# Block-sparse attention with a gated feed-forward: the first fifth of a written-out instruction order replaced, and six operations exchanged between ScalarE and VectorE

## The chip, the cores and the metric

One core of a Trainium2 chip (trn2). The metric is device time in microseconds (us) of one execution. Engines are named as in the profile: PE is TensorE (PEld its weight loads), ACT is ScalarE, DVE is VectorE, POOL is GpSimd, SP is SyncE. A name such as L757 is line 757 of the kernel.

## The reference

Four batches, 8 heads, 768 tokens, head size 64. A token block has 32 tokens, so there are 24 blocks; a mask lets a query block see its neighbours, the first and the last block, and three sampled blocks.

```python
scores = scale * np.matmul(q, k.transpose(0, 1, 3, 2))
mask = np.abs(blk_i - blk_j) <= 1
mask = mask | (blk_i == 0) | (blk_j == 0) | (blk_i == 23) | (blk_j == 23)
# ... and the three sampled key blocks of each query block
attn = softmax(np.where(mask, scores, -1e9))
x = (attn @ v), heads side by side: 768 x 512 for each batch
h = np.maximum(x @ w_in, 0.0)                 # 512 -> 1024
conv_out = 3-tap convolution of h along the tokens, weights conv_w per feature
gate = 1.0 / (1.0 + np.exp(-conv_out))
out = (h * gate) @ w_out                      # 1024 -> 512
```

## The kernel before

**Attention.** Heads are worked in pairs (P = 0 to 15, four to a batch). For each pair the transposed K and Q stand in two bf16 tiles, `e` (even token chunks) and `o` (odd ones), 64 rows of data and 24 rows of mask (rows 64 to 87), so that one matmul with 88 rows gives scores with the mask added. `e0` and `o0` are the first pair's; there are five such slots. The pairs 0 to 4 get K and Q by loads, a transpose on PE (L470 for K, L508 for Q) and copies out of PSUM by ACT (L328) or DVE (L330); later pairs by DMA transposes into `stg` and copies from there (L330). V goes through a copy `vt<-vn` into a tile with a column of ones.

The work is cut into 144 units of 8 score blocks. Each has two score steps on PE (L746, into one of two PSUM tiles `st`), one exponential on ACT (L757, `pt<-st`, 128x1024) and two steps of attention times V on PE (L779, `av<-vt,pt`). With two `st` tiles, the scores of unit u can start only after the exponential of unit u-2. After 18 units (half a batch's queries, four pairs) DVE divides (L696, L698), the result is transposed (on PE at L717 for the first half batch, by DMA later), and the feed-forward of this half batch begins.

**Feed-forward.** PE multiplies with `winb` (L895) into two small PSUM tiles `mix`; each of the 8 feature chunks of a half batch is then taken out with a relu by ACT (L915) or DVE (L917) into `hE`. DVE multiplies by the three taps (L949) and adds (L959), ACT takes a tanh (L998), DVE adds one (L1001) and multiplies by h into `gT` (L1006). PE multiplies `gT` with `woutb` (L825) into the same `mix` tiles, and DVE or ACT copies the result to `o2s` (L330, L328), from where it is stored. Transposes of K and Q, the relu and the output thus share the two `mix` tiles.

**The first microseconds.** DVE builds the mask: `nblk` (L280) and its scaled copies (L300), `hit` (L276, L284), `may` (L286), and the K rows of the mask in `e0` (L314); these rows are copied to the other head and to `o0` and the other slots (L330, 24 rows). K and Q of pair 0 come in float32 (`o2s1`, `o2s2` for the two heads' K, `o2s0` for Q in two halves) and are cast to bf16 into `nat3` (L328 on ACT or L330 on DVE, for the other engine's form). PE runs 45 matmuls without use (L1027, `warm`) before and between, and 12 later ones (L1034, fill).

**diag.** Four operations of three instructions each (L390) make diagonal matrices of the taps for two feature chunks each; only the last stretch of the kernel uses them.

**What sets the order.** The kernel makes a graph of 1789 operations and then puts them down in the order of a table of two-character numbers, `ORDER`. Where an operation may run on two engines, a letter behind its number says which (A is ACT, V is DVE); another character picks its buffer:

```python
o = ops[64 * CODE.index(line[x]) + CODE.index(line[x + 1])]
x += 2
engines = list(o.alts)
e = engines[0]
if len(engines) > 1:
    e = ENGINES[line[x]]
    x += 1
for b in o.allocs:
    b.index = CODE.index(line[x])
    x += 1
```

Each engine takes its instructions strictly in this order and waits for others through semaphores. There are no priorities at run time.

Of the kernel before, what the change touches and what calls it, by code (L numbers as in the profile page):

```python
# [17 lines left out]


ORDER = """  # L20
000x010z020B0407080905060b1e00a1f1c01q11s11801m11t1E21G21H030y0e0c0gV0d0nV0f0A0i0hA0WA30UA0oAr41r5r6r7r8r9rarb
rcrdrerfrgrhrirjrkrlrmrnrorprqrrrsrtrurvrwrx0Y01210ZA014A0VA13A0mA0XV0jV0+V0lV0t0uryrzrArBrCrDrErFrGrHrIrJrK
15017A16ArLrM4n04o0/14s14t1g11j04p00q10V0p11V1hV11lV1kV4u11dV01iV4x04yrN0rOrPrQ4C14D4z2rRrSrTrUrVrWrXrY4H04I
4E34J44q14r4v4w4Q14R4S54A4B4F4G0s0r1rV14V04W4K1u04X64+14/5071x11vV21yV1zV4L0530544T4U4Y4Z5c15d510E15505e10C1wV
4M01FV24N0F0k5h05i1I0525j21JV35m15n5o31L1561NV575811MV5r05s5f15g5w15x1KV1911n00I5t45y55F05G1bV591S30O0P0Q0R46
1A0470S481O1490T4a1U44b1V4c2404d2634e271TV34f2c14g2e04h2f4i2k24j2m11aV1oV0N1pV5H65k5l5p5q5K15L5M75u5v5z5P05Q
5A05I4O15R05U15V5W15J5a05N610625O5S5T5X5Y6324PV00J5bV5B20D5C5Z35+661675D15EV6416b06c5/0651B160V0K1DV1CV6836d4
0w0v6g16hhq0hr6i56l06m6n6ht1hu6t16uhsV0hvVhO0hQhP6v7hI0hJ6y06zhw1hxhKA6A0hyVhRhS6D16E69hz0hA6F16a1P16e6f6j6I0
6k6J6ohBA1QVhW11RVhT6q0hX6r6K26Q1hF06RhGhC1hD6S3hEAhHVhU6V06W6+11W06p06/6X47056w6x6B73074hL1hM781756hNA796C6G
7a77g06H6L6M6T17h6U6Y1Z17i07l17m6Z717276777q07r7b7n1hYhZi221XV41YVi3i4h+hV06N1i5ia36O1+Vh/ib7d21/V25V4i0ic7ei6  # L30
7s27v17w7c0ii07jio17kid7D07E7x37o7p7t7u7y7z7F4i76s1280292g12h6P7f7I17J7N07G17H7O7A37K5i17P67Biei8i92aV02bVifig
ih2dV02iV17Cijip7S17Tiq7X07Lik7U77Y7M7Q7R831847Vir7Z0851880897Wil8d18e7+8a22jVisV04k2n4l2s34mimV18002lV12tV281
iu18i08j8f38k4ix0iyizV8q18riviwViS4iTiUiV8v08wiA0iBiD1iE8s58x6iCAiFAi+0iW2o22p2qV22rV2u2002v22x2w8A18B7/08F086
878GiG08b8c8g8hiJ1iH8C78H0iXiIA8l8m8t18K18L8S08T8uiK2108yj08n1i/8oj122ViLV23Vj61j28M18U28z8X18Y8D8E8I8J90091
# [1035 lines left out]
```

## Time and profile before

| | |
|---|---|
| time, median of 3 runs | 204.63 us (204.57 to 204.76) |
| span of the profiled execution | 202.8 us, granted TensorE clock 0.998 |
| busy, share of the span | PE 97%, ACT 94%, DVE 90%, POOL 28% |
| exponentials (L757) | 144, mean 1039 ns from start to end |

The profiled execution is given by its span, from the first to the last instruction; the 1.9 us by which the timed runs are longer (204.63 less 202.76) lie around it. Busy time of an engine counts each instruction from its start to its end; neighbours on ACT and DVE overlap by about 0.1 us, and matmuls are pipelined, so a row "x8" in the timeline tells more than a mean duration. A timeline row has the start, the length, the engine, the line, the tiles (written, then read) and, in brackets, how long the engine was idle ahead of it and for whom.

### The profile page before, as it was taken

To read this page: it belongs to the slowest core of one execution; us is meant where nothing else is said; L and a number is where in the kernel's file an instruction comes from. 1 tells how busy PE (TensorE), PEld (TensorE's weight loads), DVE (VectorE), ACT (ScalarE), POOL (GpSimd) and SP (SyncE) were. 2 spreads that over 40 slices of the span, in tenths; PEclk is the share of its full clock that TensorE was granted. 3 is DMA by queue.
4 is the path that set the end of the run, shared out by engine and by line. 5 is a ranking of instruction groups with operands and counts; after the bars stand their busy time and mean duration, and the time that the engine had idled before them with its cause. 6 is when DMAs were issued, how large, how long until landed. Compare 5 with 4: busy or idle time off the path is not lost.

```text
span 202.8 us, 6814 instructions
## 1 busy us (share of the span) xinstructions
PE 196.8 (97%) x2708; PEld 153.9 (76%) x2708; DVE 181.8 (90%) x572; ACT 189.7 (94%) x251; POOL 57.5 (28%) x112
## 2 busy tenths in 40 slices
PE   7899999999999999999999999999999999999993
PEld 7799977986788777877688877876678877876742
DVE  7999989999999979999899988999899968999950
ACT  6999999999999999999999998999999989998842
POOL 8870568630520354202534328400000000000000
PEclk9999999999999999999999999999999999999999
DMA  6999999999998399956869699994321202001515
GB/s 143 177 223 207 182 135 132 167 171 151 155 122 129 61 141 154 213 106 132 133 108 159 82 197 218 135 176 115 124 72 24 41 14 68 13 10 60 204 63 202
DMA packets 53655, 25.96 MB, mean 128 GB/s; under 512 B 39616, under 2 KB 50584, under 8 KB 53624
## 3 DMA queue, kind: packets, MB, share of 16 engines
q0 software_dynamic: 19984, 11.24, 43.7%
q1 hardware_dynamic: 33208, 13.87, 34.6%
q8 instruction: 21, 0.34, 0.7%
q10 hardware_dynamic: 432, 0.43, 0.6%
q14 instruction: 10, 0.08, 0.1%
HBM read 23.08 MB, written 6.29 MB: 145 GB/s over the span
## 4 chain that ended last, share of the span: by engine, by line
PE 78%; ACT 15%; issue 3%; DVE 2%; DMA 1%; ACTq 0%
PE st L746 25%; PE mix L895 18%; PE mix L825 17%; PE av L779 14%; ACT pt L757 11%; DMA o2s<-in_k_dram 1%; DVE e L330 1%; ACT m L998 1%; PE mix L810 1%; PE st L825 1%; PE av L970 1%; ACT nat L328 1%; PE mix L508 1%; ACT hE L915 0%; ACT o2s L328 0%
## 5 line engine op out<-in xcount | busy, mean ns | idle before, releaser
L757 ACT ACTIVATE pt<-st 128x1024 bf16<-128x1024 f32 x144 | 140.6, 1039 | 1.8 <-PE st L746 0.9
L779 PE MATMUL av<-vt,pt 128*128 128x65 bf16 x1152 | 59.9, 193 | 0.2 <-DVE vt L330 0.2
L779 PEld LDWEIGHTS <-pt 128*128 128x128 bf16 x1152 | 52.3, 97 | 9.9 <-issue 0.3
L895 PE MATMUL mix<-xT,winb 128*128 128x384 bf16 (+2 forms) x288 | 53.6, 308 | 0.1
L949 DVE TENSOR_SCALAR m<-hE,cw 128x382 bf16<-128x382 bf16 (+2 forms) x192 | 49.3, 316 | 0.5 <-ACT hE L915 0.2
L825 PE MATMUL mix<-woutb,gT 128*128 128x512 bf16 x176 | 47.1, 379 | 0.3 <-DVE gT L1006 0.3
L746 PE MATMUL st<-o 88*128 88x128 bf16 (+1 forms) x240 | 43.9, 229 | 0.4 <-ACT pt L757 0.3
L746 PE MATMUL st<-o,e 88*128 88x128 bf16 (+1 forms) x228 | 43.4, 233 | 0.0
L746 PE MATMUL st<-e,o 88*128 88x128 bf16 (+1 forms) x224 | 42.3, 234 | 0.2 <-ACT pt L757 0.2
L746 PE MATMUL st<-e 88*128 88x128 bf16 (+1 forms) x208 | 40.9, 239 | 0.1
L746 PEld LDWEIGHTS <-o 88*128 88x128 bf16 x464 | 34.7, 97 | 7.7 <-issue 0.8
L746 PEld LDWEIGHTS <-e 88*128 88x128 bf16 x436 | 33.0, 97 | 7.1 <-issue 0.4
L959 DVE TENSOR_TENSOR m<-m 128x764 bf16<-128x764 bf16 (+2 forms) x64 | 33.5, 532 | 0.4
L895 PEld LDWEIGHTS <-winb 128*128 128x128 bf16 x288 | 24.0, 97 | 8.0 <-issue 0.5
L998 ACT ACTIVATE m<-m 128x764 bf16<-128x764 bf16 (+2 forms) x32 | 26.3, 829 | 0.5 <-DVE m L959 0.3
L825 PEld LDWEIGHTS <-gT 128*128 128x128 bf16 x184 | 15.0, 97 | 9.3 <-DVE gT L1006 0.5
L417 POOL COPY pace<-pt 1x1 bf16<-1x1 bf16 x24 | 6.2, 257 | 49.9 <-ACT pt L757 49.8
L1006 DVE TENSOR_TENSOR gT<-m,hE 128x764 bf16<-128x764 bf16 (+3 forms) x36 | 18.0, 510 | 0.5
L698 DVE TENSOR_TENSOR xtok<-av,rcp 128x384 bf16<-128x384 f32 (+2 forms) x36 | 18.2, 506 | 0.3
L915 ACT ACTIVATE hE<-mix 128x384 bf16<-128x384 f32 (+2 forms) x36 | 17.7, 507 | 0.7 <-PE mix L895 0.5
L240 POOL DMA_DIRECT2D nat<-in_q_dram x23 | 16.8, 733 | 3.2 <-issue 2.5
L917 DVE TENSOR_SCALAR hE<-mix 128x384 bf16<-128x384 f32 x28 | 15.3, 549 | 2.6 <-PE mix L895 2.2
(84 smaller groups left out, 157.4 us busy)
## 6 DMA issues: line engine op xcount, KB each, us to landing
out_dram<-o2s SPq DMA_DIRECT2D x23, 256.0 KB
vn<-in_v_dram POOLq DMA_DIRECT2D x16, 192.0 KB, 5.0
nat<-in_k_dram POOLq DMA_DIRECT2D x15, 192.0 KB, 4.7
nat<-in_q_dram POOLq DMA_DIRECT2D x7, 192.0 KB, 5.2
winb<-in_moe_w_in_dram POOLq DMA_DIRECT2D x2, 512.0 KB, 9.5
woutb<-in_moe_w_out_dram POOLq DMA_DIRECT2D x4, 256.0 KB, 8.2
nat<-in_q_dram POOLq DMA_DIRECT2D x8, 96.0 KB, 4.5
nq<-in_q_dram POOLq DMA_DIRECT2D x5, 96.0 KB, 5.2
```

What stands on the lines that cost most here:

```text
L240: return op(name, {eng: occ}, lambda e: on(e).dma_start(out=dst(), in_=src), prio, deps, dma=(kind, service), **kw)
L698: nm = op("norm", {"DVE": t_dps(128 * C)}, lambda e: nc.vector.tensor_tensor(out=xtok_t[xk.index][:, 0:C].rearrange("p c h d -> p h c d"), ...
L746: nc.tensor.matmul(out=st[:, 128 * x:128 * (x + n_)], lhsT=QK[kc % 2][s][0:88, 1, hh, kc // 2, :], rhs=QK[par][s][0:88, 0, hh, idx:idx + n ...
L757: nc.scalar.activation(out=pt_t[ptb.index], in_=st_t[stb.index], func=AF.Exp, bias=0.0, scale=0.125)
L779: nc.tensor.matmul(out=o[:, off:off + 65], lhsT=pt_t[ptb.index][:, 128 * x:128 * x + 128], rhs=V_t[vslot_b[P].index][:, hh, kc, 0:65], sta ...
L825: nc.tensor.matmul(out=acc(), lhsT=gT_t[gb.index][:, ffc, 128 * t:128 * t + 128], rhs=woutb[:, ffc, :], start=(ffc == 0), stop=(ffc == NFF ...
L895: nc.tensor.matmul(out=mix_t[hb.index][:, w1 * y:w1 * y + w1], lhsT=winb[:, fc, 128 * ffc:128 * ffc + 128], rhs=xT_t[xt_buf[n].index][:, f ...
L915: i = nc.scalar.activation(out=dst, in_=src, func=AF.Relu, bias=0.0, scale=0.5)
L949: i = nc.vector.tensor_scalar(out=m_t[cb.index][:, x, y, 0:w], in0=hE_t[heb.index][:, f0 + y, t0 + x:t0 + x + w], scalar1=cw[:, x, f0 + y: ...
L959: nc.vector.tensor_tensor(out=m[:, a_, :, 0:w], in0=m[:, a_, :, 0:w], in1=m[:, b_, :, 0:w], op=ALU.add)
L998: th = [op("tanh", {"ACT": t_act(2 * w) + 0.04}, lambda e, cb=cb, w=w: nc.scalar.activation(out=m_t[cb.index][:, 0, :, 0:w], in_=m_t[cb.in ...
L1006: i = nc.vector.tensor_tensor(out=gT_t[gtb.index][:, f0:f0 + 2, t0:t1], in0=m_t[cb.index][:, 0, :, 0:w], in1=hE_t[heb.index][:, f0:f0 + 2, ...
```

## The change

Fourteen rows of the table are rewritten: all that runs up to about 46 us of the program on PE and up to about 55 us on DVE. Behind that, each engine's order is the one before. POOL and SP keep their order throughout. Six operations change engine:

- from ACT to DVE: the cast of the first half of pair 0's Q (`nat3<-o2s0`), the copy of the mask rows of Q to the other head in `o0`, the copy of 128 columns of Q from PSUM (`o0<-av0`), and one relu of a 128x384 tile from PSUM (the fifth feature chunk of the first half batch, L915 before, L917 now);
- from DVE to ACT: the cast of the second head's K (`nat3<-o2s2`) and the copy of the mask rows of Q to the other head in `e0`.

Two rows of the table, before and now:

```diff
-000x010z020B0407080905060b1e00a1f1c01q11s11801m11t1E21G21H030y0e0c0gV0d0nV0f0A0i0hA0WA30UA0oAr41r5r6r7r8r9rarb
+040708090005060b1e00a1f1c01q11s1011801m11t1E20e1G2021Hr41r5r6r7r8r80hAr903rarb0gVrcrd0crerfrg0nA0drhrirj0yrkrlrm
...
```

On DVE at the start of the program, from the last step ahead of the sampled blocks to the first copies of the finished K mask (`hit`, `may`: the mask's tables; `o2s`: pair 0's K and Q in float32), before:

```order
L276 TENSOR_SCALAR hit_141<-near_142,ident24_136 24x22
L330 COPY e0_67<-e0_67 24x384
L284 TENSOR_TENSOR hit_141<-colidx_i_140,sbi_139 24x72
L286 TENSOR_REDUCE may_143<-hit_141 24x24
L370 MEMSET vt3_80 128x12
L314 TENSOR_SCALAR e0_67<-may_143 24x24x6 x2
L314 TENSOR_SCALAR e0_67<-may_143 24x8x6
L314 TENSOR_SCALAR e0_67<-may_143 24x2x8x5
L330 CAST nat3_88<-o2s2_127 128x384
L330 COPY o0_72<-e0_67 24x384
```

and of the change, the same stretch:

```order
L276 TENSOR_SCALAR hit_141<-near_142,ident24_136 24x22
L370 MEMSET vt1_78 128x12
L330 CAST nat3_88<-o2s0_125 128x192
L284 TENSOR_TENSOR hit_141<-colidx_i_140,sbi_139 24x72
L286 TENSOR_REDUCE may_143<-hit_141 24x24
L314 TENSOR_SCALAR e0_67<-may_143 24x24x6 x2
L314 TENSOR_SCALAR e0_67<-may_143 24x8x6
L314 TENSOR_SCALAR e0_67<-may_143 24x2x8x5
L330 COPY o0_72<-o0_72 24x384
L330 COPY o0_72<-e0_67 24x384
```

A cast of half of Q now stands ahead of the sampled-block steps where a mask copy stood, and behind the K mask a mask copy stands where the cast of K stood.

On ACT, from its last mask row to the first exponentials, before:

```order
L298 ACTIVATE o0_72<-nblk_138 24x256
L328 CAST nat3_88<-o2s1_126 128x384
L328 CAST nat3_88<-o2s0_125 128x192
L328 COPY o0_72<-o0_72 24x384
L328 COPY e0_67<-mix0_65 64x384
L328 COPY o0_72<-mix1_66 64x128
L328 CAST nat3_88<-o2s0_125 128x192
L328 COPY e0_67<-mix1_66 64x256
L328 COPY o0_72<-e0_67 24x384
L328 COPY o0_72<-av0_63 64x128
L328 COPY e0_67<-av0_63 64x256
L757 ACTIVATE pt0_96<-st0_61 128x1024
```

and of the change:

```order
L298 ACTIVATE o0_72<-nblk_138 24x256
L328 COPY e0_67<-e0_67 24x384
L328 CAST nat3_88<-o2s1_126 128x384
L328 CAST nat3_88<-o2s2_127 128x384
L328 COPY e0_67<-mix0_65 64x384
L328 COPY e0_67<-mix1_66 64x256
L328 COPY o0_72<-mix1_66 64x128
L328 COPY o0_72<-e0_67 24x384
L328 CAST nat3_88<-o2s0_125 128x192
L757 ACTIVATE pt0_96<-st0_61 128x1024
L328 COPY e0_67<-av0_63 64x256
L757 ACTIVATE pt1_97<-st1_62 128x1024
```

One mask copy stands ahead of the first cast, and the last copy of Q has moved behind the first exponential.

On DVE at the end of the first half batch's gates (`m3`, `gT0`: the gate of the last two feature chunks; `stg`: the next pairs' K and Q), one piece of the difference:

```order
 L330 COPY e0_67<-stg0_82 64x1536
 L330 COPY o0_72<-stg0_82 64x1536
+L390 TENSOR_SCALAR diag_131<-ident_135,cw_134 128x128 x3
 L1001 TENSOR_SCALAR m3_121<-m3_121 128x2x382
 L1006 TENSOR_TENSOR gT0_123<-m3_121,hE0_116 128x2x382
+L390 TENSOR_SCALAR diag_131<-ident_135,cw_134 128x128 x3
 L330 COPY vt0_77<-vn1_93 128x12x64
 L330 COPY e1_68<-stg1_83 64x1536
```

Two of the four diag operations stand here now; a third follows between the first two relus of the next half batch, and one is left where all four were, ahead of the first half batch's feed-forward.

More of the change, by code (lines that the diff above doesn't have):

```diff
@@ L20 @@
 ORDER = """
-000x010z020B0407080905060b1e00a1f1c01q11s11801m11t1E21G21H030y0e0c0gV0d0nV0f0A0i0hA0WA30UA0oAr41r5r6r7r8r9rarb
[L22 to L34, printed above, removed]
+040708090005060b1e00a1f1c01q11s1011801m11t1E20e1G2021Hr41r5r6r7r80hAr903rarb0gVrcrd0crerfrg0nA0drhrirj0yrkrlrm
@@ new lines @@
+0WA3rn0UV0XArorp0frqrrrsrt0i0Y00oVru1210jVrv0lV0ZA013A14Arwrx0mA0t0uryrz0/10A10VrArBrCrDrErF0VA0+V11VrG4n04orH
+rI4p0150rJrKrLrM4s117V4t16A4x04yrN00z1g11j0rO0qrP0p4u10B4z21hV14C14DrQ1kV1lVrR0x4H01dV0rS4I4q14E3rTrU4J44r1iV
+4v0s1rV14Q1rV4R4w1u04V04W4S5rW4A4B4+11vV2rX4/4X6rY1x14F0r5301yV544G1zV5074K0C5504L04T1wV4M05c11S35d4U4Y4Z0E1
+1FV25e15h00O4N5i51520F5j21I05m15n1L11JV30P0Q1NV1MV56571KV0R5815r0465s5f15g5o3591911A05w11TV35x470S485t41n01O1
+490T4a5k1U44b1V5F00K4c5G2405l5p4d2635y55q1oV4e1bV1aV5u275K15L4f5H65M75v5z2c15A04g5B22e04h5C5P02f5Q4O10k4PV05I
@@ new lines @@
+5R04i2k25J5U14j5V5N5D11pV5O2m15a05W15bV0w610620D0v5S5T5EV5X5Y661632671B16b06c5Z35+5/01DV1CV64168360V656d46g16h
+hq06i5hr6l06mhsV0ht1hu6t16u6n6hI0hJ6v76y0hvVhw16zhKAhO0hPhRhx6A0hQ6D169hyV6Ehz06F1hShThA1P1hBV6a6I06e6J6Q16f
+1QVhW16j6R1RV6K26k6ohC1hF0hX6V06S36WhG6p06+16X4hDhEA6w6/6q0705730hU74756hL16rhMhZ6xhHV6B1W0781796C6G6HhV0hYhNA
+i22i37g07h6L6Mh+6T1i51XV47a71YV6U6N16Y7i0i47l17m1Z16Z717276777b7q06O7n1ia31+V7d2ibh/1/V25V4i0ic7e7ri67s27v17w
+7c0ii07jio17kid7D07E7x37o7p7t7u7y7z7F4i76s1280292g12h6P7f7I17J7N07G17H7O7A37K5i17P67Biei8i92aV02bVif0Nigih0J
@@ L35 @@
+2dV02iV17Cijip7S17Tiq7X07Lik7U77Y7M7Q7R831847Vir7Z0851880897Wil8d18e7+8a22jVisV04k2n4l2s34mimV18002lV12tV281
+iu18i08j8f38k4ix0iyizV8q18riv0IiwViS4iTiUiV8v08wiA0iBiD1iE8s58x6iCAiFAi+0iW2o22p2qV22rV2u2002v22x2w8A18B7/08F0
+86878GiG08b8c8g8hiJ1iH8C78H0iXiIA8l8m8t18K18L8S08T8uiK2108yj08n1i/8oj122ViLV23Vj61j28M18U28z8X18Y8D8E8I8J90091
 8Z3925j38N8O08ViM1951iP0969769d08WiQiNiOA8+9e8/939i194989j998P2j7iYj8j4iZj98Qj59a3iRVja9bje29f79k1jfjgjhji9n0
```

## The prediction

> **What bounds the kernel now.** I read the page's busy shares, then the busy time by stretches, the waits, and the timelines of DVE, ACT and PE where the order changes. By stretch (columns: length, then busy time and instructions of PE, PEld, DVE, ACT, POOL, then granted clock, DMA share, GB/s):
>
> ```profile
> PE 196.8 (97%) x2708; PEld 153.9 (76%) x2708; DVE 181.8 (90%) x572; ACT 189.7 (94%) x251; POOL 57.5 (28%) x112
> 19.00:27.80 8.80, 8.80 (x157) 8.12 (x157) 7.91 (x31) 8.71 (x10) 4.79 (x11) 1.00 1.07 158
> 31.10:48.00 16.90, 16.75 (x272) 13.79 (x269) 16.68 (x50) 16.87 (x22) 8.58 (x18) 1.00 1.32 146
> 48.00:56.00 8.00, 7.86 (x92) 5.89 (x93) 7.45 (x19) 7.87 (x10) 2.54 (x5) 1.00 1.28 169
> 66.00:180.00 114.00, 113.72 (x1560) 87.00 (x1559) 105.83 (x315) 111.46 (x142) 25.51 (x48) 1.00 0.68 111
> ```
>
> From 66 to 180 us PE has 0.28 us without work in 114. Its order there is not changed, so whatever PE is late or early by at 66 us stands in the end time, one to one. The change is decided before. From 31 to 48 us three engines are full at once: DVE has 0.22 us left of 16.9, ACT 0.03, PE 0.15. From 48 to 56 DVE has 0.55 us left of 8. Who waits for whom there (engine, line, who ended it: us in total, times, longest):
>
> ```profile
> PE st L746 <- ACT pt L757: 0.4, 2, 0.3
> PE mix L825 <- DVE gT L1006: 0.3, 1, 0.3
> PE av L779 <- DVE vt L330: 0.2, 1, 0.2
> ```
>
> PE thus waits twice for DVE in the stretch that is rewritten: for the first V copy, and for a finished gate. These two waits carry my sum, and ahead of both the change gives DVE more to do.
>
> **Part 1, the start.** The chain of waits of the first 45 us runs over DVE until the first V copy is done:
>
> ```profile
> 10.65 0.58 DVE vt L330
> 11.28 0.64 PE av L779 x16
> ```
>
> The DVE timeline leading to it (start, length; in brackets idle time ahead):
>
> ```profile
> 3.25 0.25 DVE L330 COPY e<-e 24x384 bf16<-24x384 bf16 x1
> 3.97 0.22 DVE L284 TENSOR_TENSOR hit<-colidx_i,sbi 24x72 f32<-24x72 int32 x1 [0.47 <-DMA sbi<-in_sampled_blocks_dram]
> 4.61 0.85 DVE L314 TENSOR_SCALAR e<-may 24x144 bf16<-24x144 bf16 x4
> 5.49 0.62 DVE L330 CAST nat<-o2s 128x384 bf16<-128x384 f32 x1
> 9.90 0.29 DVE L330 COPY o<-mix 64x256 bf16<-64x256 bf16 x1
> 1.45 0.07 DVE L370 MEMSET vt<- 128x12 bf16 x1
> ```
>
> and that of ACT:
>
> ```profile
> 3.64 0.77 ACT L328 CAST nat<-o2s 128x384 bf16<-128x384 f32 x2
> 4.43 0.51 ACT L328 COPY o<-o 24x384 bf16<-24x384 bf16 x1
> 4.96 0.47 ACT L328 COPY e<-mix 64x384 bf16<-64x384 bf16 x1
> 5.45 0.26 ACT L328 COPY o<-mix 64x128 bf16<-64x128 bf16 x1
> 5.74 0.35 ACT L328 CAST nat<-o2s 128x192 bf16<-128x192 f32 x1
> 6.12 0.37 ACT L328 COPY e<-mix 64x256 bf16<-64x256 bf16 x1
> 7.58 4.66 ACT L757 ACTIVATE pt<-st 128x1024 bf16<-128x1024 f32 x5
> 12.40 1.02 ACT L757 ACTIVATE pt<-st 128x1024 bf16<-128x1024 f32 x1 [0.16 <-PE st L746]
> ```
>
> ACT first. Its mask rows end at about 3.6 (the cast starts at 3.64). Now a mask copy of 0.51 goes first, so the first cast starts at 4.12. Then come two casts (the pair above took 0.77 with the smaller one second; two of 384 columns 0.42 + 0.51, since the second started 0.42 behind the first), 0.47 + 0.37 + 0.26 of copies, a mask copy of 0.51, a cast of 0.35, with 0.02 between each: 4.12 + 0.93 + 0.47 + 0.37 + 0.26 + 0.51 + 0.35 + 6 x 0.02 = 7.13. The first exponential starts at about 7.15 instead of 7.58. Behind it stands the copy that left its place (0.27 from start to start), so exponentials 2 to 5 would come at 8.34, 9.25, 10.15, 11.06 (each starts some 0.91 behind the one before, from the row of five: 4.66 less the last one's 1.02, over 4), and the sixth at 11.96 instead of 12.40. On ACT alone that is a gain of 0.4 us.
>
> But the sixth needs scores that stand on PE behind the first av steps, and these need the V copy from DVE. DVE: the cast of 192 columns now stands ahead of the sampled-block step. It falls into the 0.47 us of idle time, but not wholly: ACT did this same cast as the second of its pair at about 4.06, so the data are there between 3.64 and 4.06; I take 3.8. The trace has no such cast on DVE; it lies between 0.35 (ACT, same width) and 0.62 (DVE, double width). I take 0.45, since the 0.62 is part fixed and part columns. So L284 starts at 4.25 instead of 3.97, and the mask is 0.28 later (from 0 to 0.7). From the mask's end (4.61 + 0.85 = 5.46) to the V copy's end (11.23) no row of DVE has idle time in brackets. Out of this goes the cast of K, 0.65 with its gap. Into it come the copy `o0<-o0` (0.25 as the row at 3.25, and a gap of 0.03 as between 5.46 and 5.49; the copy that it replaces lay ahead of the idle 0.47 and was free), the copy of 128 columns of Q (not on DVE in the trace; at most the 0.29 of 256 columns, at least the 0.25 of the small mask copy; 0.27) and three memsets that lay at the very start (0.05 each from start to start, 0.07 at most). Together -0.65 + 0.28 + 0.27 + 0.15 = +0.05, so the V copy ends at 11.23 + 0.28 + 0.05 = 11.56.
>
> From the start of av (11.28) to the sixth exponential (12.40) PE needed 1.12, for four av steps and two score steps; now three av, two fills and two score steps and a fill stand there, which is the same within 0.05. The sixth exponential comes at about 12.7. **Term 1: +0.3 us.** From there to the feed-forward, ACT and PE hold each other (ACT 8.71 and PE 8.80 busy of 8.80 from 19.0 to 27.8), and the sets of operations on both are the same, so I carry it in full. Ends: -0.4, if the V copy isn't late and ACT's lead counts; +0.6, if the cast waits long and costs 0.62.
>
> **Part 2, one relu from ACT to DVE.**
>
> ```profile
> L917 DVE TENSOR_SCALAR hE<-mix 128x384 bf16<-128x384 f32 x28 | 15.3, 549 | 2.6 <-PE mix L895 2.2
> L915 ACT ACTIVATE hE<-mix 128x384 bf16<-128x384 f32 x28 | 13.7, 510 | 0.1
> 31.10 0.56 DVE L917 TENSOR_SCALAR hE<-mix 128x384 bf16<-128x384 f32 x1 [0.26 <-PE mix L895]
> 48.14 0.61 PE L825 MATMUL mix<-woutb,gT 128*128 128x512 bf16 x2 [0.28 <-DVE gT L1006]
> ```
>
> ACT loses 0.37 (0.51 less the overlap), DVE gains 0.47 (the relu row at 31.10 was followed at 31.57). Both engines are full here, but PE's last wait, at 48.14, is for DVE. DVE's only idle time that the new order can use is the 0.26 ahead of 31.10: an add now stands before this relu. So the gate is 0.47 - 0.26 = 0.2 later, and PE with it. **Term 2: +0.2** (0, if the other waits of DVE give way; 0.47, if the 0.26 isn't used). What ACT is spared doesn't come forward, since the next step behind 48.14 starts when DVE has finished.
>
> The Trainium skill's page "ScalarE: Activation LUTs", under "Rules for kernel authors", says that relu belongs on VectorE, which is up to about three times faster per element in bf16. By it, the relu would cost DVE about 0.17, less than the idle 0.26, and term 2 would be 0. The two rows above differ: from float32 in PSUM, DVE takes 549 ns and ACT 510.
>
> **Part 3, three diag operations** come from a stretch in which DVE waits for others (19 to 27.8 us: 0.9 us idle) into one where it doesn't:
>
> ```profile
> 19.34 0.57 DVE L390 TENSOR_SCALAR diag<-ident,cw 128x128 bf16<-128x128 bf16 x3
> 19.85 0.29 DVE L330 COPY e<-mix 64x256 bf16<-64x256 bf16 x1
> 49.56 0.56 DVE L1006 TENSOR_TENSOR gT<-m,hE 128x764 bf16<-128x764 bf16 x1
> 51.51 1.32 DVE L330 COPY o2s<-mix 128x512 f32<-128x512 f32 x2
> 54.13 0.56 DVE L917 TENSOR_SCALAR hE<-mix 128x384 bf16<-128x384 f32 x1
> 54.90 0.56 DVE L917 TENSOR_SCALAR hE<-mix 128x384 bf16<-128x384 f32 x1 [0.21 <-PE mix L895]
> 50.51 0.59 PE L825 MATMUL mix<-woutb,gT 128*128 128x512 bf16 x2
> 52.51 0.49 PE L895 MATMUL mix<-xT,winb 128*128 128x384 bf16 x2
> ```
>
> One diag takes 0.51 (19.34 to 19.85) to 0.57; I take 0.55. The first stands ahead of the last gate: that ends at 50.12 + 0.2 + 0.55 = 50.87, and the matmul that needs it comes at 50.9 instead of 50.51 (+0.4, where term 2 is in). The second puts the output copy at 51.51 + 0.2 + 1.1, less 0.1 of small waits: 52.7 instead of 51.51, done at 53.4. It frees the `mix` tile that the matmul at 52.51 writes, which so comes at 53.45 (+0.9). The third delays the relu of 54.90 to 56.3, 1.4 late, and PE, which needs its tile, is 0.9 late by then; it waits between 0 (if it has 0.5 of slack there) and 0.5 more, and I take 0.2: +1.1 on PE. ACT, fed with scores in between, is late by 0.9. PE's wait for ACT (0.4 in two pieces, the row in the first part) can take part of it back: at 66 us, +1.0, of which term 2 is 0.2. **Term 3: +0.8.** Ends: +0.2, if PE's slack and DVE's 0.55 idle time hide most of it; +1.3, if PE can't take anything back.
>
> **Sum** on the profiled execution: 202.8 + 0.3 + 0.2 + 0.8 = 204.1; on the median, which is 1.9 longer for what lies around the span, 204.63 + 1.3 = **205.9 us**. The rest of the reordering on PE (score steps, av steps and feed-forward steps changing places by one or two) I cost at nothing: the same work stands between the same two waits for DVE; if a score step comes late there, ACT loses up to 0.3 each time.
>
> **Rivals.** *A, faster:* the start is the bound, not DVE. ACT's first exponential comes 0.4 earlier and stays so, since the V copy isn't late, and the 0.37 spared on ACT comes forward too, because ACT is as full as DVE from 31 to 48 us (16.87 of 16.90). Then 204.63 - 0.4 - 0.37 = 203.9. It decides if the V copy ends before 10.8 (the sixth exponential at 11.96 less PE's 1.12) and the diags fall into waits of DVE. For it: ACT's row is just as full. Against: idle time on DVE from 31 to 56 is 0.22 + 0.55 against 2.1 added. Chance 0.14.
>
> *B, no change:* the V copy is as early as before and PE's slack ahead of 50.51 and 52.51 takes the diags; only term 2 stays, 204.8. For it: PE's own waits for ACT can swallow a little. Chance 0.10.
>
> *C, the clock at the start, slower still:* four of the useless matmuls ahead of the first transposes have moved behind, while the first cast is 0.5 later.
>
> ```profile
> 12.85 0.44 PE st L746 x6
> 1.10 3.22 PE L1027 MATMUL st<-warm 128*128 128x128 bf16 x30 [1.10 <-DVE warm L224]
> 4.79 0.90 PE L1027 MATMUL st<-warm 128*128 128x128 bf16 x13
> 6.15 0.29 PE L508 MATMUL av<-ident,nat 128*128 128x128 bf16 x2 [0.45 <-ACT nat L328]
> ```
>
> 30 took 3.22 (0.107 each), 13 later ones 0.90 (0.06 each): the rate doubles between. Now 26 end at 3.9 and PE idles until 4.7. If the slow rate lasts through the first scores, the first exponential comes at about 8.05 (4.7, then 18 to 21 matmuls of 0.107 up to the scores, the eight score blocks of the first unit at twice the 0.44 of the first row, from the chain of waits, and 0.2 to ACT) instead of 7.15, the sixth at 12.9 instead of 12.7: 206.1. Against it: PE idled 0.45 ahead of 6.15 and kept the rate behind it (two transposes, 0.29 with the last one's tail). Chance 0.06. The Trainium skill's page "TensorE: Matmul & The Clock Gate", section "What's actually happening", has the gate open after about 3.4 us of sustained work in a window that runs freely, which leaves both open here.
>
> **How the numbers follow.** My forecast has 0.70, and 205.9 is its time. Its own range runs from 204.9 (0.3 in all) to 206.7; the lower ends of all terms together I hold unlikely. B and half of A's distance lie below; a range from 204.3 to 206.8 leaves out A and the far ends, together some 2 in 10. A measurement tells 0.2%, 0.4 us, from no change. Faster by more: A, 0.14. Within: B and the lowest forecasts, 0.11. Slower: 0.75.
>
> **What would show it.** Right: first exponential near 7.15, V copy's end near 11.55, sixth exponential near 12.7; PE's wait for gT (L825) at about 48.6 longer than 0.28; the output copies `o2s<-mix` of DVE about 1.5 us later than 51.51, and a new wait of PE at L895 for DVE's L330 or L917. Wrong: V copy before 11.2, no wait of L895 for DVE before 60 us, or PE at the scores of 66 us no later than before.

## The result: 207.3 us, 1.2% slower

The changed kernel takes 207.32 us (median; 207.13 to 207.45), the kernel before 204.6 beside it. The ratio is 1.0122, with an interval of 1.0101 to 1.0143. The profiled execution has a span of 205.41 us (205.4 on the page) against 202.76. One disturbed run of the changed kernel is left out.

| start or end, us | before | after | later by |
|---|---|---|---|
| first exponential (L757) | 7.58 | 8.27 | 0.69 |
| first V copy done (L330) | 11.22 | 12.21 | 0.99 |
| tenth / thirteenth exponential | 16.06 / 18.77 | 17.07 / 20.07 | 1.01 / 1.30 |
| first matmul of L895 | 26.96 | 28.69 | 1.73 |
| second gate done (`gT`, L1006) | 46.29 | 47.96 | 1.67 |
| first L895 behind the gates | 52.51 | 54.83 | 2.32 |
| end | 202.76 | 205.41 | 2.65 |

Read downwards: 1.0 is lost by 12 us, 0.3 near 18, 0.4 near 25, nothing from 28 to 48, 1.0 behind that. At the first stage, PE's timeline in the kernel after (start, length, engine, line, what, count; in brackets idle time ahead and who ended it):

```profile
1.07 2.95 PE L1027 MATMUL st<-warm 128*128 128x128 bf16 x26 [1.07 <-DVE warm L224]
4.71 0.50 PE L470 MATMUL mix<-ident,nat 128*128 128x128 bf16 x3 [0.69 <-ACT nat L328]
6.43 0.95 PE L1027 MATMUL st<-warm 128*128 128x128 bf16 x7
8.45 0.53 PE L1027 MATMUL st<-warm 128*128 128x128 bf16 x4
8.81 0.22 PE L746 MATMUL st<-o,e 88*128 88x128 bf16 x1
```

PE now waits 0.69 us for ScalarE's first cast, and behind that wait its matmuls are still slow: 7 take 0.95 at 6.43, where before 13 took 0.90 at 4.79. In the trace's own records of the granted clock the full rate begins at 4.02 us before and at 8.73 after. (The clock column of the profile's stretches reads 1.00 throughout; only the lengths of the matmuls show it.) What follows on ScalarE and on VectorE:

```profile
4.14 0.92 ACT L328 CAST nat<-o2s 128x384 bf16<-128x384 f32 x2
8.27 1.02 ACT L757 ACTIVATE pt<-st 128x1024 bf16<-128x1024 f32 x1 [1.00 <-PE st L746]
13.44 12.27 ACT L757 ACTIVATE pt<-st 128x1024 bf16<-128x1024 f32 x13 [0.21 <-PE st L746]
26.25 1.95 ACT L757 ACTIVATE pt<-st 128x1024 bf16<-128x1024 f32 x2 [0.54 <-PE st L746]
3.82 0.26 DVE L330 CAST nat<-o2s 128x192 bf16<-128x192 f32 x1 [0.38 <-DMA o2s<-in_q_dram]
4.59 0.85 DVE L314 TENSOR_SCALAR e<-may 24x144 bf16<-24x144 bf16 x4
8.70 0.23 DVE L330 COPY o<-av 64x128 bf16<-64x128 bf16 x1 [1.01 <-PE av L508]
11.85 0.36 DVE L330 COPY vt<-vn 128x768 bf16<-128x768 bf16 x1
```

ScalarE was ready for its first exponential at 7.26 (6.91 and 0.35) and waits 1.00 for scores. The cast that VectorE took over costs it 0.26, wholly in its idle time: the mask starts at 4.59, before at 4.61. But the Q copy that it also took over (8.70) waits 1.01 us for transposes which stand behind the slow scores, and the V copy queues behind it.

Near 25 us VectorE, then PE, and last the same transposes in the kernel before:

```profile
24.16 0.45 DVE L344 TENSOR_SCALAR mlast<-nblk 24x128 bf16<-24x128 bf16 x3
24.65 0.36 DVE L330 COPY xT<-mix 128x384 bf16<-128x384 bf16 x1
25.06 0.33 PE L717 MATMUL mix<-ident,xtok 128*128 128x128 bf16 x3 [0.41 <-DVE xT L330]
23.21 0.33 PE L717 MATMUL mix<-ident,xtok 128*128 128x128 bf16 x3
```

Three mask rows (`mlast`) stand ahead of the copy that PE waits for; in the kernel before PE has no such wait. And from 49 us on, PE and VectorE, with the stretch behind:

```profile
49.81 0.60 PE L825 MATMUL mix<-woutb,gT 128*128 128x512 bf16 x2 [0.28 <-DVE gT L1006]
50.83 0.58 DVE L390 TENSOR_SCALAR diag<-ident,cw 128x128 bf16<-128x128 bf16 x3
52.19 0.57 DVE L390 TENSOR_SCALAR diag<-ident,cw 128x128 bf16<-128x128 bf16 x3
54.11 1.26 DVE L330 COPY o2s<-mix 128x512 f32<-128x512 f32 x2
54.83 0.48 PE L895 MATMUL mix<-xT,winb 128*128 128x384 bf16 x2 [0.33 <-DVE o2s L330]
68.00:182.00 114.00, 113.67 (x1560) 86.81 (x1558) 106.22 (x315) 111.73 (x142) 25.26 (x48) 1.00 0.71 111
```

The wait at L825 is the old 0.28. The wait of L895 for the output copy is new (0.33), with two diags ahead of that copy. From 68 to 182 us PE is as full as it was (0.33 without work in 114), so what is lost by 66 us stands in the end. From the second gate to the end, the table gives 156.47 us before and 157.45 after.

### The profile page after: what moved, and what is told of

Its sections match the earlier page's. It is cut to its first block, busy times and chain, and to the rows that moved or that the text cites. A ratio compares the mean times of both kernels' runs of the same rounds, so it can differ in the third digit from the quotient of the medians.

```text
span 205.4 us, 6816 instructions
## 1 busy us (share of the span) xinstructions
PE 198.7 (97%) x2708; PEld 155.3 (76%) x2708; DVE 181.7 (88%) x574; ACT 190.1 (93%) x249; POOL 57.6 (28%) x112
## 4 chain that ended last, share of the span: by engine, by line
PE 72%; DVE 17%; ACT 7%; issue 2%; ACTq 0%
PE st L746 22%; PE mix L825 17%; PE mix L895 16%; PE av L779 12%; ACT pt L757 4%; DVE m L949 3%; DVE o L330 3%; DVE e L330 2%; DVE m L959 2%; DVE xtok L698 2%; DVE hE L917 1%; DVE diag L390 1%; DVE vt L330 1%; PE mix L810 1%; PE st L825 1%
## 5 line engine op out<-in xcount | busy, mean ns | idle before, releaser
L757 ACT ACTIVATE pt<-st 128x1024 bf16<-128x1024 f32 x144 | 141.2, 1036 | 3.9 <-PE st L746 2.9
L895 PE MATMUL mix<-xT,winb 128*128 128x384 bf16 (+2 forms) x288 | 54.1, 307 | 0.5 <-DVE o2s L330 0.3
L825 PE MATMUL mix<-woutb,gT 128*128 128x512 bf16 x176 | 47.2, 379 | 0.3 <-DVE gT L1006 0.3
L746 PE MATMUL st<-e 88*128 88x128 bf16 (+1 forms) x208 | 41.4, 241 | 0.0
L895 PEld LDWEIGHTS <-winb 128*128 128x128 bf16 x288 | 24.0, 97 | 8.4 <-issue 1.1
L825 PEld LDWEIGHTS <-gT 128*128 128x128 bf16 x184 | 15.0, 97 | 9.7 <-DVE gT L1006 0.5
L917 DVE TENSOR_SCALAR hE<-mix 128x384 bf16<-128x384 f32 x29 | 15.8, 548 | 3.4 <-PE mix L895 3.1
L1006 DVE TENSOR_TENSOR gT<-m,hE 128x764 bf16<-128x764 bf16 (+3 forms) x36 | 18.0, 511 | 0.5
L240 POOL DMA_DIRECT2D nat<-in_q_dram x23 | 17.3, 752 | 3.2 <-issue 3.0
L915 ACT ACTIVATE hE<-mix 128x384 bf16<-128x384 f32 (+2 forms) x35 | 17.1, 505 | 0.7 <-PE mix L895 0.5
```

Source lines behind the costliest of these rows:

```text
L240: return op(name, {eng: occ}, lambda e: on(e).dma_start(out=dst(), in_=src), prio, deps, dma=(kind, service), **kw)
L746: nc.tensor.matmul(out=st[:, 128 * x:128 * (x + n_)], lhsT=QK[kc % 2][s][0:88, 1, hh, kc // 2, :], rhs=QK[par][s][0:88, 0, hh, idx:idx + n ...
L757: nc.scalar.activation(out=pt_t[ptb.index], in_=st_t[stb.index], func=AF.Exp, bias=0.0, scale=0.125)
L825: nc.tensor.matmul(out=acc(), lhsT=gT_t[gb.index][:, ffc, 128 * t:128 * t + 128], rhs=woutb[:, ffc, :], start=(ffc == 0), stop=(ffc == NFF ...
L895: nc.tensor.matmul(out=mix_t[hb.index][:, w1 * y:w1 * y + w1], lhsT=winb[:, fc, 128 * ffc:128 * ffc + 128], rhs=xT_t[xt_buf[n].index][:, f ...
L917: i = nc.vector.tensor_scalar(out=dst, in0=src, scalar1=0.5, scalar2=0.0, op0=ALU.mult, op1=ALU.max)
```

## Experiments

My theory: the clock (about 1.0), orders between 12 and 28 us (0.7) and the diags (0.8 to 1.0) make the loss, the relu next to nothing. The rivals: VectorE's added load at the start; the order from 28 to 48 us. Single timings of the same kernel lay 2 us and more apart on these chips, which makes the intervals wide. Most readings therefore go by one trace of each kernel, all in one table ("full rate" from the records of the clock; times and spans in us). A ratio is taken to the kernel before, timed beside the run; medians of different runs are not compared with each other.

| run | full rate from | V copy done | first L895 | second gate done | span | ratio to before |
|---|---|---|---|---|---|---|
| before | 4.02 | 11.22 | 26.96 | 46.29 | 202.76 | |
| after | 8.73 | 12.21 | 28.69 | 47.96 | 205.41 | 1.0122 |
| after_warm30 | 4.78 | 11.04 | 27.52 | 47.52 | 204.99 | 1.0067 |
| after_diag_early | 4.59 | 11.03 | 28.79 | 48.12 | 204.65 | 1.0118 |
| after_mlast_late | 3.86 | 11.03 | 27.28 | 46.59 | 204.93 | 1.0090 |
| after_relu_act | 8.89 | 12.38 | 29.02 | 48.66 | 206.21 | 1.0139 |
| after28_before | 9.31 | 12.37 | 28.95 | 47.99 | 204.49 | 1.0054 |
| after_repaired | 5.18 | 11.53 | 27.56 | 46.98 | 203.42 | 1.0011 |
| before_warm26 | 4.19 | 10.81 | 26.72 | 46.30 | 202.76 | 1.0002 |
| before_warm20 | 10.39 | 12.58 | 28.61 | 47.79 | 204.24 | 1.0028 |
| before_diag_late | 5.38 | 11.54 | 27.28 | 46.40 | 203.87 | 1.0021 |
| before28_after | 5.35 | 11.29 | 27.02 | 46.55 | 203.00 | 0.9994 |
| before_relu_dve | 5.92 | 11.28 | 27.02 | 46.43 | 204.90 | 0.9995 |
| start_after_rest_before | 3.76 | 10.95 | 27.02 | 46.14 | 203.25 | 1.0007 |

### The clock

**Four warm-up matmuls put back (after_warm30).** On PE:

```diff
-warm (L1027) x26
+warm (L1027) x30
 k_tr (L470), then q_tr (L508), the other warm matmuls between and behind them
```

> The kernel after, with four of the warm-up matmuls that the change moved behind the first transposes put back ahead of them: 30 there instead of 26, the rest as in the kernel after. Clock theory: PE then works until the 0.060 us rate is granted (about 4.0 us), the seven warm-up matmuls behind the transposes take about 0.4 instead of 0.75 to 0.95, and the first score block comes near 6.1, the first exponential near 7.2 instead of 8.27, the first V copy ends near 11.2 to 11.6 instead of 12.21; the time is 0.6 to 1.0 us below the 207.3 of the kernel after. Rival, VectorE's own load at the start delays the V copy whatever PE's rate: the first exponential comes earlier, but the V copy still ends near 12.1 and the time stays within 0.2 of 207.3. Second rival, the gap ahead of the first transpose (PE waits there for ScalarE's cast until 4.7) undoes the rate again with 30 as with 26: nothing changes.

PE, then ScalarE:

```profile
1.07 3.38 PE L1027 MATMUL st<-warm 128*128 128x128 bf16 x30 [1.07 <-DVE warm L224]
4.70 0.36 PE L470 MATMUL mix<-ident,nat 128*128 128x128 bf16 x3 [0.25 <-ACT nat L328]
5.51 0.55 PE L1027 MATMUL st<-warm 128*128 128x128 bf16 x7
7.06 1.02 ACT L757 ACTIVATE pt<-st 128x1024 bf16<-128x1024 f32 x1
```

The milestones came as the clock theory said: seven matmuls in 0.55, first exponential at 7.06, V copy at 11.04, 1.17 earlier than in the kernel after and even earlier than in the kernel before. So VectorE's added load does not delay the V copy; the first rival falls. The timed loss fell from 1.22% to 0.67% (206.79 us; ratio 1.0067, interval 1.0036 to 1.0099). That is about 1.1 us, but the two intervals allow 0.4 to 1.9. The span fell by only 0.42: in this trace only 0.44 of the 1.17 was left at the second gate. Where the rest went in it stands in the last section.

after_diag_early and after_mlast_late have the 26 warm-up matmuls and the pause of the kernel after and got the full rate at 4.59 and 3.86, all the same. So the pause does not always cost the rate: in a single trace the moment of the grant is partly luck.

**Fewer warm-up matmuls in the kernel before**, 26 and then 20 ahead of the transposes:

```diff
-warm (L1027) x30
+warm (L1027) x26      (before_warm26)     or x20     (before_warm20)
 k_tr, q_tr
-warm x13
+warm x17                                  or x23
```

> The kernel before, with only 26 warm-up matmuls ahead of the first transposes and four more behind them; all else as before. Clock theory in its simple form (PE idle for a few tenths of a us just ahead of the grant at 4.0 is enough to put the grant off to about 8.7): the first exponential comes near 8.3 instead of 7.58, and the time is 0.6 to 1.0 us above 204.6. Rival: here the first transpose stands ready at 4.4 instead of 4.7, the pause is only about 0.5 us, and the rate comes at 4.0 to 4.5 as before: the time is 204.6 within 0.2.

> The kernel before with 20 warm-up matmuls ahead of the first transposes and ten more behind them, so that PE pauses there for about 0.9 to 1.0 us, as in the kernel after. Theory, a grant of the full rate needs a stretch of 3.41 us, laid by a clock that runs freely, with less than some 0.85 us of pause in it: then some executions get it by 4.7 us and run at 204.6, the others (the larger part) between 8 and 10.5 us with the first V copy 0.9 to 1.2 later and the time 0.3 to 1.1 longer. The kernel before keeps its order behind, so VectorE's slack up to its second gate may take part of it back. Rival, the late grant belongs to the order of the kernel after and not to the pause: the grant is at 4 to 5.4 us and the time that of the kernel before, within 0.2.

With 26 nothing changed (205.08 us, ratio 1.0002, interval 0.9973 to 1.0032; full rate at 4.19): the first transpose is ready at 4.17 there, so there is hardly a pause. With 20:

```profile
4.17 0.50 PE L470 MATMUL mix<-ident,nat 128*128 128x128 bf16 x3 [0.75 <-ACT nat L328]
4.96 2.63 PE L1027 MATMUL st<-warm 128*128 128x128 bf16 x23
8.91 1.02 ACT L757 ACTIVATE pt<-st 128x1024 bf16<-128x1024 f32 x1 [0.43 <-PE st L746]
```

PE pauses 0.75 us, 23 matmuls take 2.63, the full rate comes at 10.39, and the V copy is 1.36 late. The span is 1.48 longer; the median is 205.95 us, and the ratio 1.0028 (0.9998 to 1.0058) cannot tell that from no change by itself. The order of the kernel after isn't needed for a late rate: in this execution the pause was enough. Over the fourteen traces: where PE waits 0.25 us or less for ScalarE ahead of the first transposes, the rate comes between 3.76 and 5.92 (eight traces); where it waits 0.68 to 0.75, at 3.86 and 4.59, or at 8.73, 8.89, 9.31 and 10.39.

### The stretch from 12 to 28 us

**The mask rows behind the copies (after_mlast_late).** On VectorE:

```diff
-mlast (L344) x3
 x_cp: xT<-mix (L330)
 q_cp
 x_cp: xT<-mix (L330)
+mlast (L344) x3
```

> The kernel after, with one VectorE operation moved: the three mask rows of mlast (0.46 us together) stand behind the first two copies of the transposed attention output (xT) instead of ahead of the first. Theory, PE's wait of 0.41 for VectorE's xT copy near 24 us, and the 0.43 that the exponentials lose there, come from mlast: the wait goes (below 0.1), and the first feed-forward matmul comes 0.4 us earlier against the sixth exponential than in the kernel after (15.25 behind it there). The time falls by 0.4, or by less if VectorE is what sets the pace from 30 to 48 us. Rival, the wait is for the normalisation that stands ahead of the copies and not for mlast: the wait stays above 0.3 and the time is unchanged.

On PE:

```profile
23.30 0.33 PE L717 MATMUL mix<-ident,xtok 128*128 128x128 bf16 x3
25.74 0.40 PE L508 MATMUL mix<-ident,nq 128*128 128x128 bf16 x4 [0.30 <-DMA nq<-in_q_dram]
```

The wait for VectorE is gone, and the first L895 comes 15.02 behind the sixth exponential (12.26) instead of 15.25 (28.69 less 13.44; in after_warm30 15.26). The exponential nearest to it, the twentieth, gains the whole 0.47 against after_warm30. PE gives half of that back by 28 us, because it waits 0.30 for a load of Q at 25.74. In after_repaired below, with the same move, that half stays: its first L895 comes 8.16 behind the thirteenth exponential, against 8.62 in the kernel after and 8.19 before. VectorE's second gate is 0.93 earlier than in after_warm30. Then VectorE waits:

```profile
49.22 0.55 DVE L330 COPY e<-stg 64x1536 bf16<-64x1536 bf16 x1 [0.84 <-DMA stg<-nat]
```

The staged K and Q are not there, and the fourth gate comes when it came in after_warm30 (51.8). 207.33 us, ratio 1.0090 (1.0059 to 1.0121). The profiled execution itself took 206.69 us; three of the twelve timings lie at 205.6 to 205.9, about where the profiled one would be without that wait, though nothing shows that these three lacked it. So the theory holds at 25 us, and the timing doesn't show it.

### The two halves

**Before up to 28 us, then after (before28_after), and the reverse (after28_before).** The order is cut at the first relu (L917):

```diff
-operations of the kernel after up to the first relu
+operations of the kernel before up to the first relu
 what is left, in the order of the kernel after      (after28_before: the two exchanged)
```

> The kernel before up to its first relu (about 28 us), then what is left of the operations in the order of the kernel after, three diag operations excepted that the kernel before has already done by then, and with the relu on VectorE. So it holds the change's middle without its start and without the moved diags. Theory, the start and the stretch to 28 us cost about 1.7 of the 2.65 us on the span and the diags 0.7 to 1.1: the time is within 0.3 of the 204.6 of the kernel before. Rival, the order from 28 to 48 us has a cost of its own on VectorE (the relu, 0.47, and multiplies that are longer beside the DMA issues of GpSimd) which the late start hid: 205.0 to 205.6.

> The kernel after up to its first relu (about 28 us), then what is left of the operations in the order of the kernel before, but with the relu on VectorE and with three diag operations still to be done, right behind that point. Theory, what is lost by 28 us stays: 0.6 us over the kernel before when PE's full rate comes by 5 us, 1.7 when it comes near 8.7, and the three diags, about 1.6 us of VectorE, are partly hidden in VectorE's waits for the first relus (1.6 us in the kernel after): 205.2 to 206.6. Rival, the loss of the start is recovered by 48 us because VectorE is ahead of its work there: 204.6 to 205.0.

The second half without the moved diags, and with the relu on VectorE, costs 0.24 on the span, of which 0.06 was there at the first L895 (204.67 us, ratio 0.9994, 0.9959 to 1.0029). In the trace the rival's 0.4 to 1.0 us are not there; the timing alone would still allow 0.6. The first half costs 1.99 at the first L895, and 1.73 of it stays to the end (206.26 us, ratio 1.0054, 1.0025 to 1.0083); its full rate came at 9.31. Other than its expectation says, the relu stands on ScalarE in after28_before. Behind its first half the three diags cost nothing that can be seen: they stand where VectorE waits for PE's first L895.

### The diags

**The three diags late, alone (before_diag_late).** On VectorE, at the three places that the kernel after has:

```diff
-diag (L390) x3, three times between 19 and 27 us
 stg_cp, stg_cp
+diag x3
 g1, g2 (third step's gate)
+diag x3
 ...
 relu (L917)
+diag x3
 relu (L917)
```

> The kernel before, with nothing changed but the places of three diag operations of VectorE: from the stretch of 19 to 27 us to the places that they have in the kernel after (two around 50 us, one around 57 us). The prediction's third term says +0.8 us (204.6 becomes 205.4; bounds +0.2 and +1.3), with a matmul of L825 0.4 late at the first and one of L895 waiting for VectorE's output copy about 0.3 and coming 0.9 late at the second. Rival, PE's slack there hides them and the loss of the kernel after past 48 us has another cause: 204.6 within 0.2.

VectorE, then PE:

```profile
50.63 0.57 DVE L390 TENSOR_SCALAR diag<-ident,cw 128x128 bf16<-128x128 bf16 x3
52.55 1.27 DVE L330 COPY o2s<-mix 128x512 f32<-128x512 f32 x2
53.27 0.48 PE L895 MATMUL mix<-xT,winb 128*128 128x384 bf16 x2 [0.33 <-DVE o2s L330]
```

The span is 1.11 longer, and the wait of 0.33 is the one foreseen. The V copy was 0.32 late already (full rate at 5.38), but at the second gate only 0.11 of that was left. The other 1.00 comes behind it: from the second gate to the end it takes 157.47 us. In the other traces that stretch takes 157.45 to 157.55 with the diags late, and 156.44 to 156.53 with them early; the three in which VectorE waits 0.8 us or more for the staging are left out. So the diags cost 1.0 there, in either order. Timed: 205.52 us, ratio 1.0021 (0.9996 to 1.0046), which allows up to 0.9 us and doesn't tell the cost from none.

**The diags early again in the kernel after (after_diag_early).** The same edit backwards, with the kernel before's places:

> The kernel after, with the three diag operations put back to the places that they have among VectorE's operations in the kernel before (from 19 to 27 us). Theory, the diags cost 0.65 to 0.95 us where they stand now and little there: 206.4 to 206.7. Rival, in the kernel after VectorE is itself what PE waits for at 24 us (PE's transposes of the attention output wait 0.41 for its copy), so the diags cost there about what they cost at 50 us: 207.3 within 0.3.

The trace bears out the mechanism of the rival. PE's share in the stretches (length, then PE's busy time) of after_warm30, and of this run, with the same early rate:

```profile
19.00:24.00 5.00, 4.59 (x89) 4.32 (x87) 4.78 (x17) 5.00 (x7) 1.65 (x4) 1.00 1.27 203
24.00:28.00 4.00, 3.98 (x68) 3.57 (x67) 2.55 (x10) 3.45 (x5) 3.22 (x8) 1.00 0.85 109
19.00:24.00 5.00, 4.32 (x84) 4.03 (x82) 4.84 (x20) 4.61 (x5) 1.55 (x3) 1.00 1.23 199
24.00:28.00 4.00, 3.20 (x57) 2.81 (x56) 3.18 (x16) 2.68 (x3) 3.11 (x8) 1.00 0.82 111
```

PE loses 1.48 there instead of 0.43. The first L895 is 1.27 later than in after_warm30, and nothing more is lost behind 48 us (156.53 from the second gate to the end). The span ends 0.34 below that of after_warm30. The timings are too wide to tell (207.63 us, ratio 1.0118, 1.0063 to 1.0173), and the profiled execution, at 206.41, lies where the first theory put it. In the order of the kernel after, VectorE doesn't have the time for three diags at 20 us either.

### The relu

**Back on ScalarE in the kernel after (after_relu_act), and on VectorE in the kernel before (before_relu_dve).**

```diff
 relu of 128x384, VectorE's fourth in the kernel after (at 34.13)
-  VectorE, tensor_scalar (L917)
+  ScalarE, activation (L915)          (before_relu_dve: the reverse)
```

> The kernel after, with the one relu of 128x384 back on ScalarE, in the same place of the order. The prediction's second term says -0.2 us (0 to -0.47) against the kernel after. Theory from the comparison of the runs, VectorE runs without a pause from about 30 us to the second gate (near 47.9), so that the gate comes 0.47 us earlier if VectorE sets the pace there, and the time falls by 0.2 to 0.5. Rival, the late start of PE hides the relu (the gate was no later against PE's first feed-forward matmul in the kernel after than before, 19.27 against 19.33): unchanged within 0.1.

> The kernel before with one relu of 128x384 moved from ScalarE to VectorE and nothing else: the prediction's second term by itself. The prediction: +0.2 us (0 to +0.47), since VectorE has no idle time from 31 us to its second gate (46.29), which would come up to 0.47 later. Theory after the runs so far (with this relu back on ScalarE the kernel after lost 0.46 between PE's first feed-forward matmul and the end): ScalarE is the tighter of the two, and the time is 0.2 to 0.45 below that of the kernel before.

In the order of the kernel after, ScalarE with the relu (after_relu_act) and without it (after), then VectorE with the relu on ScalarE:

```profile
34.72 0.84 ACT L998 ACTIVATE m<-m 128x764 bf16<-128x764 bf16 x1
35.45 0.49 ACT L915 ACTIVATE hE<-mix 128x384 bf16<-128x384 f32 x1
35.82 1.95 ACT L757 ACTIVATE pt<-st 128x1024 bf16<-128x1024 f32 x2
34.39 0.84 ACT L998 ACTIVATE m<-m 128x764 bf16<-128x764 bf16 x1
35.12 3.08 ACT L757 ACTIVATE pt<-st 128x1024 bf16<-128x1024 f32 x3
35.98 0.32 DVE L949 TENSOR_SCALAR m<-hE,cw 128x382 bf16<-128x382 bf16 x1 [0.66 <-ACT hE L915]
```

The 31st exponential is 0.83 later than in the kernel after, and 0.33 of that was there at 29 us (28.69 to 29.02); the rest, 0.5, is the relu's own length. VectorE, spared 0.47, then waits 0.66 for this relu, and the second gate comes 19.64 behind the first L895 instead of 19.27. So VectorE gains nothing from giving the relu away, contrary to the prediction and to my theory. What it is worth at the end isn't shown. The span is 0.47 longer behind the first L895, but after_warm30, with the relu on VectorE, is 0.75 longer there than the kernel after, and its second gate comes 20.00 behind the first L895. The timings don't tell either: 207.95 us, ratio 1.0139 (1.0109 to 1.0169), beside 1.0122 (1.0101 to 1.0143). In the kernel before the move changes nothing up to the second gate (0.14 late, 0.06 of it from the start). What comes after that can't be read, since VectorE waits twice for the staging DMA:

```profile
49.05 0.55 DVE L330 COPY e<-stg 64x1536 bf16<-64x1536 bf16 x1 [0.82 <-DMA stg<-nat]
52.62 0.67 DVE L330 COPY e<-stg 64x1536 bf16<-64x1536 bf16 x1 [1.18 <-DMA stg<-nat]
```

205.54 us, ratio 0.9995 (0.9966 to 1.0023).

### Three causes undone, and a mixture

**after_repaired.**

```diff
-PE: warm x26, then k_tr
+PE: warm x38, then k_tr
-VectorE: mlast ahead of the first xT copy
+VectorE: mlast behind the second xT copy
-VectorE: three diags near 50.8, 52.2 and 57.2 us
+VectorE: three diags ahead of the first relu (L917)
```

> The kernel after with three things undone in its own order, the six exchanged operations left as the change has them: 38 warm-up matmuls instead of 26 ahead of the first transposes (no pause of PE there), the mask rows of mlast behind the first two xT copies, and the three late diag operations ahead of VectorE's first relu, where it waits 1.05 and 0.53 us in the kernel after. Theory, these three are the whole loss: first exponential near 7.1, PE's first feed-forward matmul at most 0.4 later than in the kernel before, no wait of PE for VectorE's output copies near 54 us, and the time is 204.6 to 205.1. Rival, ScalarE and PE lose as much again from 28 to 60 us, or VectorE then waits for the staged K and Q (0.84 us near 49 us, when mlast alone was moved): 205.5 or more.

VectorE at the place of the diags:

```profile
27.43 1.72 DVE L390 TENSOR_SCALAR diag<-ident,cw 128x128 bf16<-128x128 bf16 x9
28.92 1.15 DVE L917 TENSOR_SCALAR hE<-mix 128x384 bf16<-128x384 f32 x2
```

205.24 us, ratio 1.0011 (0.9981 to 1.0042): of the 1.2%, about 0.1% is left, and nothing that the timing can tell from the kernel before. On the span 1.99 of 2.65 is gone. What is left, 0.66, is there at the first L895 (0.60) already: 38 slow matmuls hold the first transpose back to 5.09 (V copy 0.31 late), and the exponentials lose 0.3 between the tenth and the thirteenth as in the kernel after. The diags, 1.72 us of work, cost nothing that can be seen. The six exchanged operations are in this kernel, so their exchange is not the loss.

**start_after_rest_before**, made to beat both kernels: the start of the kernel after without a loss of the clock, then the order of the kernel before.

```diff
 PE: warm x38 ahead of k_tr; VectorE: two memsets (L370) behind the first V copy
 operations of the kernel after up to about 15 us
-what is left, in the order of the kernel after
+what is left, in the order of the kernel before
```

> The start of the kernel after (up to about 15 us, with five of the six exchanged operations, 38 warm-up matmuls ahead of the first transposes, and two of the memsets for V moved behind the first V copy), then the order of the kernel before; the relu on ScalarE. Theory, ScalarE's lead of 0.5 us at the first exponential and the earlier V copy leave 0.15 to 0.3 us at PE's first feed-forward matmul, and VectorE's full stretch up to the second gate takes it back: 204.6 within 0.3. Rival, the lead stays: 204.2 to 204.4, faster than both kernels.

The lead at the V copy (0.27) is lost by the tenth exponential (0.09 late there), the second gate is 0.15 early, and then VectorE waits for the staging DMA:

```profile
51.23 0.55 DVE L330 COPY e<-stg 64x1536 bf16<-64x1536 bf16 x1 [1.00 <-DMA stg<-nat]
```

205.42 us, ratio 1.0007 (0.9976 to 1.0037). No version beat the kernel before by more than can be told.

## Why the prediction was wrong

The sign was right, the size half of what came: +1.3 forecast, +2.7 measured, outside the range. The steps that failed are the start, priced without the slow clock, and the rest of the reordering, put at nothing.

**Term 1, the start (+0.3): mis-sized.** It measured 1.0 by the V copy and 1.73 by 28 us, and its parts failed one by one. The delay of the mask by 0.28 did not come, because the cast of 192 columns takes 0.26 and not 0.45; with an early rate the V copy ends at 11.03, not at 11.56. What came in its place was rival C, to which I gave 0.06. The failed step is the sentence against it: that PE idled 0.45 ahead of 6.15 and kept the rate. That pause lay behind the grant (4.02), the new one lies ahead of it, and the runs show that there a pause can cost another 4 to 6 us of slow rate. C's own price was too low too (first exponential 8.05, sixth 12.9; measured 8.27 and 13.44): I priced the scores, and not the Q copy on VectorE, which waits 1.01 for transposes behind them with the V copy in its queue.

**"The rest of the reordering ... I cost at nothing": 0.7 us.** 0.4 of it is `mlast` ahead of the xT copy, shown by moving it twice. I looked at who PE waits for in the old order, and not at what the new order puts ahead of those copies. The other 0.3, between the tenth and the thirteenth exponential, is there in every kernel with the first half of the kernel after; PE is full there in both kernels (5.00 busy of 5.00 from 14 to 19 us after, 4.92 before), so I take it for steps of PE that come earlier. That wasn't tried by itself.

**Term 2, the relu (+0.2): not seen.** The gate's wait stayed 0.28, and the second gate came 19.27 behind the first L895 instead of 19.33. In the six traces with the order of the kernel before from there on and the relu on ScalarE this distance is 19.04 to 19.58, so 0.2 lies within what it varies by. The step that failed is that a relu on VectorE is added work there and nothing else. In the new order VectorE would wait 0.66 for the same relu on ScalarE (after_relu_act), so on VectorE it takes the place of a wait. VectorE's larger waits, for its first two relus in the kernel after,

```profile
29.54 0.56 DVE L917 TENSOR_SCALAR hE<-mix 128x384 bf16<-128x384 f32 x1 [1.05 <-PE mix L895]
30.64 0.56 DVE L917 TENSOR_SCALAR hE<-mix 128x384 bf16<-128x384 f32 x1 [0.53 <-PE mix L895]
```

end before the moved relu (34.13) and can't pay for it; they are the place where after_repaired puts the diags. "What ACT is spared doesn't come forward" stays open: without the relu ScalarE's 31st exponential comes 0.3 to 0.5 earlier in the new order (10.75 to 10.96 behind the first L895 in six traces, 11.25 in after_relu_act), and no run tells what is left of it at the end. The Trainium skill's page "ScalarE: Activation LUTs" advises relu on VectorE under "Rules for kernel authors". The trace of after_relu_act agrees for this relu, though not for the reason of speed that the page gives: 549 ns on VectorE, 510 on ScalarE before.

**Term 3, the diags (+0.8): right.** In the traces they cost 1.00 by themselves, with the new wait of L895 for the output copies, as foreseen. In the kernel after, the lateness grows by 0.98 from the second gate to the end.

Adding up on the span: 0.99 + 0.31 + 0.43 - 0.06 + 0.98 = 2.65, from the rows of the table (the fourth number is what is regained up to the second gate). This says where the lateness arose, not what each cause is worth alone: undoing the first of them alone gave 0.42 on the span, and undoing three together 1.99.

## What to carry to other kernels

Before an order is changed at the start, look at what keeps TensorE busy until its clock comes: with a pause of some 0.7 us ahead of the grant the rate came some 4 to 6 us late in four traces of six, and without it in none of eight. In the kernel after that cost 1.2 us at the first V copy, and four useless matmuls more shortened the pause to 0.25. Price an order by what it newly puts ahead of the operations that others wait for, and place loose work where its engine waits for somebody (the three diags: 1.0 us late, nothing to be seen ahead of the first relu). And a gain at the start of a kernel with several full engines need not reach the end: in one trace 1.17 us became 0.42.

## What the runs showed of the hardware

**The full rate comes in steps.** The stretches at full rate in the traces' clock records are 194.56, 197.97 or 201.39 us long, 3.41 and 3.42 apart. The Trainium skill's page "TensorE: Matmul & The Clock Gate", section "What's actually happening", describes a freely running window of 3.413 us, which these lengths agree with. It gives the spread of the transition as half a microsecond to either side; here it lay between 3.76 and 10.39 us. That a window with a pause in it can be refused would explain the late ones; it is inferred from these traces. How much pause a window bears is not settled: 2.8 us of work in one of 3.41 seems to have been too little in before_warm20, and about as much enough in after_mlast_late.

**VectorE's bf16 multiplies stretch beside DMA issues of GpSimd.** The same operation on VectorE and the issue next to it on GpSimd, in after_warm30 and then in the kernel after:

```profile
35.42 0.63 DVE L1001 TENSOR_SCALAR m<-m 128x764 bf16<-128x764 bf16 x1
35.13 0.76 POOL L240 DMA_DIRECT2D nat<-in_q_dram  x1 [0.24 <-issue]
36.37 0.32 DVE L1001 TENSOR_SCALAR m<-m 128x764 bf16<-128x764 bf16 x1
36.74 0.76 POOL L240 DMA_DIRECT2D nat<-in_q_dram  x1 [0.27 <-issue]
```

0.63 beside an issue, 0.32 without one. Not every multiply beside an issue stretches: in after_warm30 one at 38.53 lies wholly beside an issue and takes 0.31. The ten stretched ones between 29 and 48 us in the traces of before, after and after_warm30 all end just behind the end of an issue, by 0.06 us (0.16 for the two of double width), as if held until then. Four multiplies are 0.2 to 0.3 longer in after_warm30, three are 0.1 longer in the kernel after; that is most of the 0.73 by which VectorE takes longer from its second relu to the second gate (29.47 to 47.52, against 30.64 to 47.96), and so of the gain at the start that was lost. The Trainium skill's page "SBUF — State Buffer", section "Who interferes with whom", has VectorE in its faster modes and GpSimd exclude each other at a shared port; the rows agree, but no run took the issues away to show it.

**The staging varies from trace to trace.** VectorE's wait for the staged K and Q near 50 us is 0 in the traces of both kernels, and 0.2 to 2.0 us in total in five of the twelve experiments, among them before_warm26, whose order there is that of the kernel before. What decides it stays open.
